# Linear attention feeding a SwiGLU block: group 0's second layer ends tile by tile, batch 1's small matmuls are gathered, batch 1's tail moves into group 1, and one eviction moves to ScalarE

## The chip, the cores and the metric

One NeuronCore of one Trainium2 chip runs the whole program. The metric is device microseconds (us) of one execution; lower is better. Where a ratio is given with an interval, it is a 95% interval.

## The reference, cut to what matters

```python
# q, k, v: 8 batches x 8 heads x 576 positions x 64, float32
q_p, k_p = phi(q), phi(k)                       # phi(x) = elu(x) + 1
kv  = einsum('bhsd,bhse->bhde', k_p, v)         # one 64 x 64 matrix per head
z   = sum(k_p, axis=2)
num = einsum('bhsd,bhde->bhse', q_p, kv)
den = einsum('bhsd,bhd->bhs', q_p, z) + 1e-6
x   = (num / den)  -> 4608 tokens x 512
out = (silu(x @ w_gate) * (x @ w_val)) @ w_out  # 512 -> 1536 -> 512
```

## The kernel before: the parts that matter

The 4608 tokens are worked in nine groups of 512 (`g` = 0 to 8). A group has a *first layer* (12 blocks `fb`, each four gate and four value matmuls of 128x128 by 512 columns) and a *second layer* (four output tiles `t` of 12 matmuls each, evicted from PSUM by ScalarE, "A", or VectorE, "V"). Between these large matmuls the attention of the coming group is done with small ones. A batch has nine blocks of 64 positions and a group takes eight, so group 0 has the first eight blocks of batch 0, group 1 the last of batch 0 and the first seven of batch 1, and the last two blocks of batch 1, its **tail**, belong to group 2.

PSUM is used as four pairs of banks that go round in a ring. `corners` computes numerators (with `R`, the k.v matrices) or denominators (with `Zr`, the sums of k) for a stretch of blocks, as 64x64 matmuls. `kv_corner` computes k.v, `r_copy` copies it out of PSUM into `R`. `lnrd` makes the reciprocal of the denominators on ScalarE (log, then exponential of its negative). `xmul` multiplies numerators by it and writes `xT`, the input of the first layer.

```python
def corners(ps, W, b, lp, j0, j1, c0):           # 4 small matmuls a call
    for l2 in range(2):
        rows = slice(D * l2, D * l2 + D)
        for hh in range(2):
            nc.tensor.matmul(out=ps[l2][C*hh:C*hh+C, c0:c0 + C*(j1-j0)],
                             lhsT=W[rows, lp, hh, :], rhs=qt(b, lp, hh, j0, j1)[rows], ...)
def kv_corner(b, lp, t, first, last):            # 36 matmuls into columns D*lp .. D*lp+63 of BOTH banks
    ...
def block(g):                                    # ahead of the last tile of a group's second layer
    ...
    for lp in range(2):
        num(b1, lp)                              # numerators of the next group
        x_copy(b1, lp, "AV", 2 * C if b1 == 2 else 0)
    if b2 < B:
        kv_all(b2)
        r_copy(b2, 0, 2, "AA")
    ...
def layer2_0():                                  # group 0's second layer, batch 1's attention in between
    ...                                          # dz, cq: the two free pairs of banks
    def s5(): kvr(0)                             # kvr(lp): kv_corner(1, lp), then r_copy of it on VectorE
    def s6(): kvr(1); nx(0, cq)                  # nx: numerators into the pair, then xmul to xT
    def s7():
        nx(1, dz)
        for lp in range(2):                      # the tail of batch 1
            corners(cq, Zr[1], 1, lp, 7, 9, P * lp)
            corners(cq, R[1], 1, lp, 7, 9, 256 + P * lp)
        ...
    step = {1: [s0], 3: [s1, s3], 6: [s2], 7: [s4], 9: [s5], 10: [s6], 11: [s7]}
    for fb in range(FB):                         # all four tiles advance together
        for f in step.get(fb, []): f()
        for t in range(4): l2_mm(0, t, fb)
    s8()                                         # four evictions in a row on VectorE, then the tail's xmul
# group 1 and later, second layer:
for t in range(4):
    ...
    lay2(g, t)
    l2_out(g, t, "AV"[t % 2])                    # tile 1: VectorE
```
(cut and shortened; `...` marks cuts)

## Time and profile before

The median is 319.05 us (318.77 to 319.06, three runs). TensorE is busy 97% of the span.

The first view is a table of windows of the kernel before: one row per stretch, with its length, then the busy time of TensorE (PE), its weight loads (PEld), VectorE (DVE), ScalarE (ACT) and GpSimd (POOL), the granted clock, the DMA share (which this view can print above 1) and the rate. I put the cuts at four marks of the PE timeline: the start of group 0's second layer, of group 1's first layer, of group 1's second layer, and of group 2's first layer.

```profile
core 0: us, PE busy (x) PEld busy (x) DVE busy (x) ACT busy (x) POOL busy (x), PEclk, DMA share, GB/s
39.46:54.59 15.13, 15.05 (x211) 6.85 (x210) 9.36 (x21) 11.46 (x17) 7.10 (x11) 1.00 1.22 206
54.59:75.42 20.83, 20.83 (x98) 9.49 (x97) 20.52 (x38) 11.74 (x20) 3.80 (x6) 1.00 1.09 210
75.42:89.41 13.99, 12.95 (x202) 6.42 (x201) 10.89 (x20) 8.29 (x13) 0.00 (x0) 1.00 0.44 89
89.41:318.50 229.09, 224.93 (x1402) 104.41 (x1399) 141.33 (x231) 95.87 (x149) 14.47 (x21) 1.00 0.36 71
```

One reading aid: PE's ends are modelled and matmuls overlap, so I count a piece of work from its start to the next start. Four large matmuls then take 0.86 us.

Next, the waits of PE from 38 to 92 us in the kernel before (who waited, for whom: total, times, longest).

```profile
PE pp L252 <- DVE osb L320: 1.0, 1, 1.0
```

And the PE timeline of the kernel before around the places that the change touches (start, length, line, operands, shape, count; in brackets the idle time before it and what ended it). L297 is the second layer, L290 the first, L183 k.v, L252 the corners.

```profile
49.85 0.48 PE L183 MATMUL pp<-vr,kp 64*64 64x64 f16 x36
50.26 1.04 PE L297 MATMUL pp<-wo,hT 128*128 128x512 f16 x4
51.23 0.48 PE L183 MATMUL pp<-vr,kp 64*64 64x64 f16 x36
51.53 0.40 PE L252 MATMUL pp<-qT,R 64*64 64x64 f16 x8
51.86 1.04 PE L297 MATMUL pp<-wo,hT 128*128 128x512 f16 x4
52.83 0.42 PE L252 MATMUL pp<-qT,R 64*64 64x64 f16 x8
53.07 0.55 PE L252 MATMUL pp<-qT,Zr 64*64 64x128 f16 x4
53.38 0.29 PE L252 MATMUL pp<-qT,R 64*64 64x128 f16 x4
...
53.72 1.04 PE L297 MATMUL pp<-wo,hT 128*128 128x512 f16 x4
54.59 1.02 PE L290 MATMUL pp<-xT,wg 128*128 128x512 f16 x4
...
84.12 0.51 PE L252 MATMUL pp<-qT,R 64*64 64x384 f16 x6
85.67 0.35 PE L252 MATMUL pp<-qT,R 64*64 64x384 f16 x2 [1.04 <-DVE osb L320]
85.68 1.09 PE L183 MATMUL pp<-vr,kp 64*64 64x64 f16 x72
86.70 2.76 PE L297 MATMUL pp<-wo,hT 128*128 128x512 f16 x12
```

Two things are worth seeing. From 50.26 to 51.23 stand four large matmuls in 0.97 us instead of 0.86: each insertion of small work costs about 0.1 us on top of itself. And the block in group 1 takes 2.58 us (84.12 to 86.70), with a hold of 1.04 us until VectorE has evicted output tile 1, whose pair of banks the numerators of the second half are to go into.

### The profile page before, as it was taken

To read this page: it belongs to the slowest core of one execution; us is meant where nothing else is said; L and a number is where in the kernel's file an instruction comes from. 1 tells how busy PE (TensorE), PEld (TensorE's weight loads), DVE (VectorE), ACT (ScalarE), POOL (GpSimd) and SP (SyncE) were. 2 spreads that over 40 slices of the span, in tenths; PEclk is the share of its full clock that TensorE was granted. 3 is DMA by queue.
4 is the path that set the end of the run, shared out by engine and by line. 5 is a ranking of instruction groups with operands and counts; after the bars stand their busy time and mean duration, and the time that the engine had idled before them with its cause. 6 is when DMAs were issued, how large, how long until landed. Compare 5 with 4: busy or idle time off the path is not lost.

```text
span 318.5 us, 5777 instructions
## 1 busy us (share of the span) xinstructions
PE 309.6 (97%) x2315; PEld 147.7 (46%) x2315; DVE 203.7 (64%) x354; ACT 150.8 (47%) x227; POOL 48.4 (15%) x73
## 2 busy tenths in 40 slices
PE   8799999999899999999999999999999999999994
PEld 7544444444444454444444454445444444444443
DVE  3654875999849874988499739973992343234320
ACT  3764859737543474347533753385331333133311
POOL 8565344400000050006000600000000000000000
PEclk9989999999999999999999999999999999999999
DMA  8999999994430389038903790215013400140014
GB/s 158 193 198 199 206 207 206 244 225 89 93 78 3 74 117 234 5 76 119 236 2 67 114 236 16 51 31 127 2 37 70 101 0 2 34 100 0 2 33 99
DMA packets 41163, 32.52 MB, mean 102 GB/s; under 512 B 16432, under 2 KB 36400, under 8 KB 41136
## 3 DMA queue, kind: packets, MB, share of 16 engines
q0 software_dynamic: 20736, 18.58, 37.6%
q1 hardware_dynamic: 20320, 13.51, 17.8%
q8 instruction: 18, 0.29, 0.4%
q10 hardware_dynamic: 80, 0.07, 0.1%
q14 instruction: 9, 0.07, 0.1%
HBM read 37.75 MB, written 9.44 MB: 148 GB/s over the span
## 4 chain that ended last, share of the span: by engine, by line
PE 89%; DVE 5%; DMA 3%; issue 1%; POOL 1%; ACT 0%; POOLq 0%; DVEq 0%
PE pp L290 55%; PE pp L297 27%; DMA vr<-in_v_dram 3%; PE pp L183 2%; PE pp L252 2%; PE pp L274 1%; DVE hT L283 1%; DVE den L218 1%; DVE qp L227 1%; PE pp L122 1%; DVE kp L157 0%; POOL kr L101 0%; DVE prod L214 0%; DVE osb L320 0%; PE pp L368 0%
## 5 line engine op out<-in xcount | busy, mean ns | idle before, releaser
L118 ACT ACTIVATE sil<-pp 128x512 f16<-128x512 f32 x108 | 63.3, 597 | 102.8 <-PE pp L290 97.9
L290 PE MATMUL pp<-xT,wg 128*128 128x512 f16 x424 | 108.9, 380 | 0.0
L290 PE MATMUL pp<-xT,wv 128*128 128x512 f16 x424 | 108.9, 380 | 0.0
L283 DVE SCALAR_TENSOR_TENSOR hT<-pp,sil 128x512 f16<-128x512 f32 x108 | 72.0, 681 | 47.4 <-PE pp L290 34.3
L297 PE MATMUL pp<-wo,hT 128*128 128x512 f16 (+1 forms) x444 | 97.5, 374 | 0.5 <-DVE osb L320 0.5
L297 PEld LDWEIGHTS <-hT 128*128 128x128 f16 x444 | 42.1, 98 | 48.8 <-issue 1.9
L290 PEld LDWEIGHTS <-wv 128*128 128x128 f16 x424 | 41.4, 98 | 50.1
L290 PEld LDWEIGHTS <-wg 128*128 128x128 f16 x424 | 41.4, 98 | 49.4
L320 DVE TENSOR_SCALAR osb<-pp 128x512 f32<-128x512 f32 (+1 forms) x20 | 13.2, 674 | 31.4 <-PE pp L297 31.4
L118 ACT ACTIVATE osb<-pp 128x512 f32<-128x512 f32 (+1 forms) x17 | 9.8, 578 | 34.9 <-PE pp L297 34.9
L118 ACT ACT_TABLE_LOAD x14 | 18.0, 1283 | 2.8 <-PE pp L290 2.6
L118 ACT ACTIVATE ek<-kr 128x1152 f16<-128x1152 f16 x16 | 17.8, 1155 | 0.3 <-DMA kr<-in_k_dram 0.3
L644 POOL COPY gate<-qT 128x1 f16<-128x1 f16 x4 | 1.4, 359 | 102.4 <-DVE hT L283 75.8
L227 DVE TENSOR_TENSOR qp<-qp,rden 128x1152 f16<-128x1152 f16 x12 | 16.2, 1347 | 0.0
L218 DVE TENSOR_REDUCE den<-prod 128x18 f32<-128x1152 f16 x12 | 16.1, 1343 | 0.0
L118 ACT ACTIVATE eq<-qr 128x1152 f16<-128x1152 f16 x12 | 13.2, 1147 | 0.0
L269 DVE TENSOR_SCALAR xT<-pp 128x512 f16<-128x512 f32 (+1 forms) x14 | 8.8, 667 | 6.8 <-PE pp L252 6.8
L101 POOL DMA_DIRECT2D vr<-in_v_dram x16 | 11.7, 734 | 6.6 <-DMA wo<-in_moe_w_out_dram 1.9
L101 POOL DMA_DIRECT2D kr<-in_k_dram x16 | 11.5, 720 | 6.6 <-DMA wo<-in_moe_w_out_dram 1.9
L101 POOL DMA_DIRECT2D qr<-in_q_dram x15 | 10.9, 731 | 8.5 <-DMA vr<-in_v_dram 2.5
L145 DVE TENSOR_SCALAR ek<-ek 128x1152 f16<-128x1152 f16 x16 | 7.5, 471 | 5.4 <-ACT ek L118 5.4
L157 DVE TENSOR_TENSOR kp<-ek,kp 128x1152 f16<-128x1152 f16 x14 | 10.6, 758 | 0.5
(66 smaller groups left out, 180.6 us busy)
## 6 DMA issues: line engine op xcount, KB each, us to landing
out_dram<-osb SPq DMA_DIRECT2D x70, 128.0 KB, 3.3
kr<-in_k_dram POOLq DMA_DIRECT2D x16, 288.0 KB, 6.7
vr<-in_v_dram POOLq DMA_DIRECT2D x16, 288.0 KB, 10.2
qr<-in_q_dram POOLq DMA_DIRECT2D x15, 288.0 KB, 12.5
wo<-in_moe_w_out_dram POOLq DMA_DIRECT2D x3, 512.0 KB, 13.0
wg<-in_moe_w_gate_dram POOLq DMA_DIRECT2D x5, 256.0 KB, 9.4
wv<-in_moe_w_val_dram POOLq DMA_DIRECT2D x5, 256.0 KB, 9.9
q<-in_q_dram SPq DMA_DIRECT2D x1, 576.0 KB, 3.7
```

The lines of the kernel that those rows point to most:

```text
L101: nc.gpsimd.dma_start(out=dst[b % NB][:, 2 * lp:2 * lp + 2, :], in_=src[b].rearrange("(l a) (c j) d -> (a c) l (j d)", a=2, j=J)[:, 2 * lp ...
L118: nc.scalar.activation(out=out, in_=in_, func=func, bias=bias, scale=scale)
L145: nc.vector.tensor_scalar(out=a, in0=a, scalar1=1.0, scalar2=None, op0=ALU.min)
L157: nc.vector.tensor_tensor(out=a, in0=ek[b % 2][:, lp, :, :], in1=a, op=ALU.add)
L183: nc.tensor.matmul(out=ps[hh][D * l2:D * l2 + D, D * lp:D * lp + D], lhsT=t[b % 2][rows, lp, j, D * l2:D * l2 + D], rhs=vr[b % NB][rows, 2 ...
L218: nc.vector.tensor_reduce(out=den[:, c, :], in_=prod[:, :, :].rearrange("p j (l d) -> p (j l) d", d=D), axis=AX.X, op=ALU.add)
L227: nc.vector.tensor_tensor(out=qv, in0=qv, in1=rden[:, c, :].unsqueeze(2).to_broadcast([P, 2 * J, D]), op=ALU.mult)
L269: nc.vector.tensor_scalar(out=dst, in0=ps[l2][:, c0:], scalar1=1.0 / SC, scalar2=None, op0=ALU.mult)
L283: nc.vector.scalar_tensor_tensor(out=hT[g % 2][:, fb, :], in0=ps[1][:, :], scalar=SC, in1=s[:, :], op0=ALU.mult, op1=ALU.mult)
L290: nc.tensor.matmul(out=ps[h][:, :], lhsT=w[:, c, P * fb:P * fb + P], rhs=xT[g % 2][:, c, :], start=(c == 0), stop=(c == 3))
L297: nc.tensor.matmul(out=l2p[(g, t)][:, n0:n1], lhsT=hT[g % 2][:, fb, P * t:P * t + P], rhs=wo[:, fb, n0:n1], start=(fb == 0), stop=(fb == F ...
L320: nc.vector.tensor_scalar(out=o[:, n0:n1], in0=ps[:, n0:n1], scalar1=1.0 / SC, scalar2=None, op0=ALU.mult)
```

## The change

The intent: end group 0's output tiles one after the other, so that their evictions spread and PSUM pairs come free early; join the two denominators of batch 1 and its two k.v halves, for fewer insertions; open group 1 with two chunks of `xT` for two pairs of banks, so that the second half of `xT` may come later; move batch 1's tail out of group 0 into the block of group 1; and evict tile 1 of group 1 on ScalarE. The tail needs a log there, so the table set with log and exponential is named for that layer.

The diff in full:

```diff
--- before.py
+++ after.py
@@ -520,10 +520,21 @@
         if b1 < NG:
             for lp in range(2):
                 num(b1, lp)
+                if b1 == 2:
+                    corners(nump[(2, lp)], R[1], 1, lp, 7, 9, 0)
                 x_copy(b1, lp, "AV", 2 * C if b1 == 2 else 0)
         if b2 < B:
             kv_all(b2)
+            if b1 == 2:
+                for lp in range(2):
+                    corners(kvp[b2], Zr[1], 1, lp, 7, 9, 2 * P + P * lp)
             r_copy(b2, 0, 2, "AA")
+            if b1 == 2:
+                lnrd(kvp[b2], 0, 2 * P, 4 * P)
+                for lp in range(2):
+                    for l2 in range(2):
+                        w0 = 2 * P + P * lp
+                        xmul(xT[0][:, 2 * lp + l2, 0:P], nump[(2, lp)][l2][:, 0:P], rd[0][:, l2, w0:w0 + P])
         put_off(l2p[(g, "p", 1)])
 
     def layer2_0():
@@ -559,53 +570,41 @@
                 for b in range(2):
                     p8[b][f]()
 
-        def s2():
-            den(0, dz)
-
         def s3():
             qtr(1, 1, cq[1])
             for f in pm[1]:
                 f()
 
         def s4():
+            den(0, dz)
             den(1, cq)
 
-        def s5():
-            kvr(0)
-
-        def s6():
-            kvr(1)
-            nx(0, cq)
-
-        def s7():
-            nx(1, dz)
-            for lp in range(2):
-                corners(cq, Zr[1], 1, lp, 7, 9, P * lp)
-                corners(cq, R[1], 1, lp, 7, 9, 256 + P * lp)
-            exp_k(2, 0)
-            exp_k(2, 1)
-            lnrd(cq, 0, 0, 256)
-
-        def s8():
-            for t in range(4):
-                l2_out(0, t, "V")
-            for l2 in range(2):
-                xmul(xT[0][:, l2::2, 0:P], cq[l2][:, 256:512].rearrange("p (l c) -> p l c", l=2),
-                     rd[0][:, l2, 0:256].rearrange("p (l c) -> p l c", l=2))
-
-        step = {1: [s0], 3: [s1, s3], 6: [s2], 7: [s4], 9: [s5], 10: [s6], 11: [s7]}
-        for fb in range(FB):
-            if fb in step:
-                for f in step[fb]:
-                    f()
+        step = {1: [s0], 3: [s1, s3], 7: [s4]}
+        FO = 8
+        for fb in range(FO):
+            for f in step.get(fb, []):
+                f()
             for t in range(4):
                 l2_mm(0, t, fb)
-        s8()
+        for t in range(4):
+            if t == 2:
+                kvr(0)
+                kvr(1)
+            if t == 3:
+                nx(0, dz)
+            for fb in range(FO, FB):
+                l2_mm(0, t, fb)
+            if t < 3:
+                l2_out(0, t, "V")
+        nx(1, cq)
+        exp_k(2, 0)
+        exp_k(2, 1)
+        l2_out(0, 3, "V")
         exp_q(2, 0)
         exp_q(2, 1)
         phi_k(2, 0)
         phi_k(2, 1)
-        ring[:] = [dz, l2p[(0, "p", 0)], l2p[(0, "p", 1)], cq]
+        ring[:] = [l2p[(0, "p", 0)], dz, cq, l2p[(0, "p", 1)]]
 
     for g in range(NG):
         b1, b2 = g + 1, g + 2
@@ -636,7 +635,15 @@
                     ld2(k, kr, 2)
                     ld2(q, qr, 2)
                     ld2(v, vr, 2)
-            l1(g, fb)
+            if g == 1 and fb < 2:
+                if fb == 0:
+                    two = [pair(), pair()]
+                    for cs in ((0, 1), (2, 3)):
+                        for i in range(2):
+                            l1_mm(g, i, two[i], cs)
+                l1_post(g, fb, two[fb])
+            else:
+                l1(g, fb)
             for f in sl[fb]:
                 f()
         if g + 3 < B:
@@ -654,6 +661,8 @@
                 f()
             for t in range(4):
                 if t == 0 and b2 < B:
+                    if g == 1:
+                        nc.scalar.preload_act_table_set("natural_log_exp_and_others")
                     exp_k(b2, 0)
                     exp_k(b2, 1)
                     exp_q(b2, 0)
@@ -675,7 +684,7 @@
                         o = l2_out(g, t, "V" if n0 == 0 else "A", n0, n1, o)
                     continue
                 lay2(g, t)
-                l2_out(g, t, "AV"[t % 2])
+                l2_out(g, t, "A" if g == 1 and t == 1 else "AV"[t % 2])
             if b2 < B:
                 zb(b2)
```

## The prediction

> **What bounds the kernel.** TensorE. The page has PE busy 97% of 318.5 us; in the timeline four 512-column matmuls repeat every 0.86 us at a granted clock of 1.0. From group 1 on, the table of waits lists only two PE waits: 1.0 us (numerator matmuls of group 2, for an output eviction on VectorE at 84.94) and 0.5 us at the very end. Only PE time outside the large matmuls can be won.
>
> **What the change touches, from the PE timeline.**
>
> 1. Group 0's second layer, 39.46 to 54.59, takes 15.1 us, of which 48 large matmuls are 10.4. The rest is small work in seven insertions, each with about 0.1 us extra when large matmuls resume. The Trainium skill ("TensorEngine Tiling (Array Packing)", Key Properties: mode switching requires a drain) fits: the weight-load row shows 0.42 us of "issue" before each small block. The last insertion (52.83 to 53.72, 0.89 us) contains the 16 tail corners of batch 1, with a hold of 0.38 us that the chain of waits follows to VectorE's xT multiplication, because the corners reuse the bank it reads.
> The change leaves six insertions, joins the denominators and the k.v blocks, and moves the tail away: 0.89 becomes about 0.36, one switch saves 0.1, joining saves 0.1. Estimate -0.7 us. The reordered evictions should not stall PE: by my walk the first half of xT is ready at 53.5 and 54.2 against its use at 53.9 and 54.3, the second at 54.8 and 55.4 against 55.6. That fits only because group 1 opens with two chunks of two pairs; margins are 0.1 to 0.8 us.
>
> 2. The block in group 1's layer 2 (84.12 to 86.70) takes 2.58 us; its sibling in the next group (118.00 to 119.22) takes 1.22. The difference is the 1.04 wait plus a slower k.v run after it. Evicting tile 1 on ScalarE, idle then, removes the wait: -1.3 us.
>
> 3. The moved corners return in this block as 16 matmuls of 64x64x128: by the sibling's 0.46 us for 16 corners, +0.4 us.
>
> 4. New ScalarE work there (two logs and two exponentials of 256 columns, 1.75 us by the earlier trace) and four VectorE multiplications (about 0.27 each) run under the last 12 large matmuls (2.7 us) and end about when group 2's first layer starts, each chunk just in time (margin 0.2 to 0.6). Cost 0 expected, up to 0.5.
>
> 5. The named table load costs nothing: the exponentials needed one load there anyway (1.28 us in the trace). The Trainium skill ("ScalarE: Activation LUTs", Table sets) says that set has both exp and ln, so the later log needs no second one.
>
> Later groups are unchanged and PE-dense, so the shift persists: -0.7 -1.3 +0.4 = -1.6 us; I allow 0.1 for small holds.
>
> **Prediction.** 317.4 us, range 316.7 to 318.3. Faster by over 2%: 0.01; within 2%: 0.98; slower by over 2%: 0.01.
>
> **What would show each step.** Group 1's first layer starts near 53.9 instead of 54.59 (1). PE's wait for the eviction is gone, and the block spans about 1.6 us (2, 3). Group 2's first layer begins near 87.9 instead of 89.41, without a PE wait for xT (4). Table loads stay 15 (5).
>
> **What would make it wrong.** A table load inserted around the late log; xT chunks late at either opening; R copies on VectorE queued behind evictions, holding batch 1's numerators; bank reuse at group 2's start waiting for the last multiplications. Each costs 0.3 to 1.5 us and brings the time back toward 318 to 319. If VectorE's backlog in group 1 was itself delaying PE, the gain could reach 2.2.

## The result, and the profile after

The kernel after takes 317.2 us (317.1 to 317.46, four runs) against 318.91 us (318.47 to 319.06, four runs); the ratio is 0.995 [0.9933, 0.9967]. A ratio is the mean time of one kernel's fast runs over that of the other's of the same rounds, so not quite the ratio of the medians quoted.

The windows of the kernel after, cut at the same four marks:

```profile
36.98:52.45 15.47, 14.85 (x195) 6.88 (x194) 9.90 (x21) 10.66 (x15) 6.42 (x9) 1.00 1.22 207
52.45:73.29 20.84, 20.84 (x102) 9.52 (x98) 20.53 (x37) 10.98 (x18) 5.24 (x8) 1.00 1.19 227
73.29:86.19 12.90, 12.90 (x218) 6.48 (x217) 10.56 (x22) 10.21 (x18) 0.00 (x0) 1.00 0.62 112
86.19:315.30 229.11, 224.95 (x1402) 104.49 (x1400) 141.52 (x232) 95.98 (x149) 14.24 (x21) 1.00 0.36 70
```

The waits of PE from 38 to 92 us in the kernel after:

```profile
PE pp L183 <- DVE R L199: 0.5, 1, 0.5
```

The PE timeline of the kernel after at the places that answer to those shown of before (L274 is the two-chunk opening of group 1's first layer):

```profile
40.39 0.72 PE L376 MATMUL pp<-id,qr 128*64 128x128 f16 x8
40.94 0.61 PE L368 MATMUL pp<-id,qr 128*64 128x128 f16 x16
41.48 3.63 PE L297 MATMUL pp<-wo,hT 128*128 128x512 f16 x16
...
48.30 0.48 PE L183 MATMUL pp<-vr,kp 64*64 64x64 f16 x36
49.28 0.60 PE L183 MATMUL pp<-vr,kp 64*64 64x64 f16 x36 [0.51 <-DVE R L199]
49.82 1.04 PE L297 MATMUL pp<-wo,hT 128*128 128x512 f16 x4
50.79 0.42 PE L252 MATMUL pp<-qT,R 64*64 64x64 f16 x8
51.14 1.04 PE L297 MATMUL pp<-wo,hT 128*128 128x512 f16 x4
52.10 0.41 PE L252 MATMUL pp<-qT,R 64*64 64x64 f16 x8
52.45 0.39 PE L274 MATMUL pp<-xT,wg 128*128 128x512 f16 x1
...
82.09 0.63 PE L252 MATMUL pp<-qT,R 64*64 64x384 f16 x16
82.55 0.83 PE L183 MATMUL pp<-vr,kp 64*64 64x64 f16 x72
83.20 0.30 PE L252 MATMUL pp<-qT,Zr 64*64 64x128 f16 x8
83.43 2.76 PE L297 MATMUL pp<-wo,hT 128*128 128x512 f16 x12
```

The surprise is in the first row. Group 0's second layer, which was to lose 0.7 us, is 0.34 us *longer* (15.47 against 15.13). The gain inside the windows is all in group 1's second layer (13.99 to 12.90), where the wait for the eviction is gone. The other 2.5 us of the difference between the two spans lie before the first mark, in a part of the program whose order of instructions is identical in both. So two questions stood open: what of the time is the change's at all, and what ate the gain in group 0. The new wait of 0.51 us between the two k.v halves is the suspect for the second.

### The profile page after: what moved, and what is told of

Same layout as the page of the kernel before. It is cut to its first block, busy times and chain, and to the rows that moved or that the text cites. A ratio compares the mean times of both kernels' runs of the same rounds, so it can differ in the third digit from the quotient of the medians.

```text
span 315.3 us, 5774 instructions
## 1 busy us (share of the span) xinstructions
PE 307.6 (98%) x2315; PEld 146.9 (47%) x2315; DVE 204.7 (65%) x355; ACT 151.2 (48%) x228; POOL 48.3 (15%) x73
## 4 chain that ended last, share of the span: by engine, by line
PE 85%; DMA 10%; POOL 2%; issue 1%; DVE 0%; ACT 0%; POOLq 0%; DVEq 0%
PE pp L290 51%; PE pp L297 29%; DMA qr<-in_q_dram 4%; DMA kr<-in_k_dram 3%; DMA vr<-in_v_dram 3%; PE pp L252 2%; PE pp L183 1%; PE pp L274 1%; POOL wg L110 0%; POOL wv L110 0%; POOL kr L101 0%; DVE osb L320 0%; POOL qr L101 0%; POOL vr L101 0%; PE pp L210 0%
## 5 line engine op out<-in xcount | busy, mean ns | idle before, releaser
L290 PE MATMUL pp<-xT,wg 128*128 128x512 f16 x416 | 106.8, 379 | 0.0
L290 PE MATMUL pp<-xT,wv 128*128 128x512 f16 x416 | 106.8, 379 | 0.0
L290 PEld LDWEIGHTS <-wv 128*128 128x128 f16 x416 | 40.7, 98 | 49.1
L290 PEld LDWEIGHTS <-wg 128*128 128x128 f16 x416 | 40.6, 98 | 48.6 <-DVE xT L406 0.3
L118 ACT ACT_TABLE_LOAD x13 | 16.7, 1283 | 2.3 <-PE pp L290 2.1
```

What stands on the lines that cost most here:

```text
L118: nc.scalar.activation(out=out, in_=in_, func=func, bias=bias, scale=scale)
L290: nc.tensor.matmul(out=ps[h][:, :], lhsT=w[:, c, P * fb:P * fb + P], rhs=xT[g % 2][:, c, :], start=(c == 0), stop=(c == 3))
```

## The experiments

Twelve runs were made, each with five rounds beside the kernel before on the same chip; two of them repeat the two kernels, and e8 repeats e4. All results were correct. The table has what each came to: time, the ratio to before, and the two stages that the change touches. "q wait" is by how much the stretch of transposes in group 0's layer (the pieces L376 and L368 after the first eight large matmuls) exceeds the 0.79 us it takes when undisturbed; "net" is the layer without it.

| run | time, us | ratio to before | group 0, layer 2 | q wait | net | group 1, layer 2 |
|---|---|---|---|---|---|---|
| first trace of before | 319.05 | | 15.13 | 0 | 15.13 | 13.99 |
| first trace of after | 317.2 | 0.995 [0.9933, 0.9967] | 15.47 | 0.30 | 15.17 | 12.90 |
| c1_before | 318.36 | 0.9987 [0.9965, 1.0009] | 15.13 | 0 | 15.13 | 14.09 |
| c2_after | 317.42 | 0.9957 [0.9935, 0.9978] | 15.17 | 0 | 15.17 | 12.91 |
| e1_evict | 316.92 | 0.9942 [0.9919, 0.9964] | 15.59 | 0.47 | 15.12 | 12.66 |
| e2_tail | 318.11 | 0.9976 [0.9951, 1.0002] | 15.10 | 0.51 | 14.59 | 14.30 |
| e3_noevict | 318.13 | 0.9998 [0.9974, 1.0022] | 15.17 | 0 | 15.17 | 13.64 |
| e4_join | 316.46 | 0.9937 [0.992, 0.9953] | 14.39 | 0.01 | 14.38 | 12.92 |
| e5_plain | 318.3 | 1.001 [0.998, 1.004] | 15.17 | 0 | 15.17 | 12.92 |
| e6_tailevict | 316.69 | 0.9942 [0.9924, 0.9959] | 14.59 | 0 | 14.59 | 12.86 |
| e7_rfirst | 316.97 | 0.9952 [0.9938, 0.9966] | 15.57 | 0.52 | 15.05 | 12.91 |
| e8_join_again | 316.7 | 0.9943 [0.9931, 0.9956] | 14.46 | 0.09 | 14.37 | 12.93 |
| e9_join_qearly | 316.19 | 0.9928 [0.9915, 0.994] | 14.38 | 0 | 14.38 | 12.89 |
| e10_apart | 316.58 | 0.9952 [0.9927, 0.9977] | 14.60 | 0 | 14.60 | 12.90 |

The medians of before were 318.63 (the c runs, e1, e2), 318.56 (e3 to e6), 318.53 (e7 to e9) and 318.38 us (e10). Single runs of one kernel mostly spread over 0.4 to 1.4 us, and a few stand up to 2.4 us above their median (320.76 among the runs of before, for instance), so intervals are as wide as most of the effects here. The six that stand highest are also the six with the lowest mean granted clock, 0.994 or 0.995 where the others have 0.997 to 1.0. They enter the means, so they move ratios: e5 has two of them, e3 and e10 one each, and before has one beside e3 to e6. The stage lengths are far steadier: group 1's first layer is 20.83 to 20.85 us in every trace but e5, and the rest after group 2's opening 229.1 to 229.2. I therefore take the times as a check and decide by stages.

### c1_before and c2_after: both kernels again

The edit is none.

> The kernel before once more, as a control. My theory of where the two traces differ: the first 37 to 39 us are the same program in both, so the 2.5 us by which the first trace of before reaches group 0's second layer later (39.46 against 36.98) is scatter of the loads, not the change. If so, this trace begins that layer somewhere between 36.9 and 39.5, and the layer lasts 15.1 to 15.5 us, the longer the earlier it begins (a wait for the second q load of batch 1, which lands near 40.8). Rival: the change did speed the beginning; then this trace again begins the layer near 39.4. Time 318.5 to 319.1.

> The kernel after once more. Theory: group 0's second layer lasts 15.4 to 15.5 us again if the wait for the copy of R (0.5 us) is part of the program, and the block in group 1 about 1.35 us. The beginning scatters as in the other control. Rival (the change sped the beginning): it begins the layer at 37.0 again while the control of before does not. Time 317.0 to 317.5, ratio 0.995.

Before begins group 0's second layer at 37.53 us this time, not at 39.46, and after at 37.48 instead of 36.98. So the beginning is scatter, and two things made up the 2.5 us. The first trace of before held PE for 1.2 us there for a load of v, and the new one has no such wait. And for some 3 us the clock granted to TensorE was half, as the windows view of the first trace of before shows:

```profile
15.10:18.18 3.08, 3.08 (x86) 1.68 (x85) 1.29 (x2) 2.34 (x4) 2.70 (x4) 0.50 1.45 198
```

The same matmuls take 1.81 us at a clock of 1.00 in the first trace of after (13.95 to 15.76), and 1.81 us in c1. No run shows why the clock was lower. In all twelve experiments the layer begins between 37.09 and 37.55. Comparing the first two spans (318.5 and 315.3) would have credited the change with 2 us that are not its own. The rival is out.

The stage readings repeat: 15.13 and 14.09 for before, 15.17 and 12.91 for after. Group 0's layer is 15.17 us without a wait for q, and the 0.30 us more in the first trace of after were that wait. In this pair the medians differ by 0.94 us and the stages by 1.14.

### e1_evict: only the eviction of tile 1

```diff
 # kernel before
-                l2_out(g, t, "AV"[t % 2])
+                l2_out(g, t, "A" if g == 1 and t == 1 else "AV"[t % 2])
```

> Before with only the eviction of tile 1 in group 1 moved to ScalarE. My theory: the numerator matmuls no longer wait, the block falls from 2.58 to about 1.25 us and the time by 1.1 to 1.3 us (ratio about 0.996). Rival: VectorE's backlog is what holds, so the wait moves to the next thing that VectorE delivers (the x copies) and the gain is under 0.5 us.

In the PE timeline of this run the eight matmuls of the numerators go through without a hold:

```profile
82.42 0.52 PE L252 MATMUL pp<-qT,R 64*64 64x384 f16 x8
```

The block falls from 2.58 to 1.12 us (82.42 to 83.54), with no wait in it, and the layer from 14.09 to 12.66. The median is 316.92 us, 1.7 under before; the layer accounts for 1.4 of that. This one line thus does all that the whole change does: in the same call the change itself measured 317.42. The rival, that the wait would move on to VectorE's copies, is out.

### e2_tail: only the move of the tail

```diff
 # kernel before
         def s7():
             nx(1, dz)
-            for lp in range(2):
-                corners(cq, Zr[1], 1, lp, 7, 9, P * lp)
-                corners(cq, R[1], 1, lp, 7, 9, 256 + P * lp)
             exp_k(2, 0)
             exp_k(2, 1)
-            lnrd(cq, 0, 0, 256)
 # s8: without the tail's xmul; block() and the table load as in the change
```

> Before with only the tail of batch 1 moved into group 1's block (and the named table load), group 0's layer otherwise as before, tile 1 still evicted on VectorE. Theory: group 0's layer loses the 0.38 us hold and 0.2 us of corners, so about 0.5 us shorter; the block in group 1 gains 0.3 to 0.4 us of corners; the wait for the eviction shrinks from 1.04 towards 0.4 because VectorE starts group 1 without 0.75 us of multiplications. Total -0.3 to -0.9 us. Rival: the tail only changes place and its cost stays; total within 0.2 us of before.

Group 0's layer sheds 0.54 us net (15.13 to 14.59), a little over the 0.5 expected. Group 1's layer gets 0.21 longer (14.30 against 14.09). The wait for the eviction did not shrink as I had expected; it is still 1.0 us, although VectorE's multiplications for the tail are gone from group 1's beginning. VectorE ends its sums ahead of that eviction 9.70 us after the layer's start in this trace, as in c1. The median is half a microsecond under before, and the interval reaches 1.

### e3_noevict: the change without the eviction

```diff
 # kernel after
-                l2_out(g, t, "A" if g == 1 and t == 1 else "AV"[t % 2])
+                l2_out(g, t, "AV"[t % 2])
```

> After with tile 1 of group 1 evicted on VectorE again. Theory: VectorE's queue is what the eviction waits in; in the traces of after VectorE ends its sums 0.6 us sooner relative to the layer's start than before, so the wait comes back only in part: about 0.5 us, layer 2 of group 1 about 13.4 us (12.9 in after, 14.0 before), time +0.5 us against after. Rival (the eviction is worth 1.3 us wherever it stands): 14.2 us and +1.3.

The wait is back, but shorter, as the PE timeline of this run shows:

```profile
83.12 0.35 PE L252 MATMUL pp<-qT,R 64*64 64x384 f16 x4 [0.31 <-DVE osb L320]
```

Group 1's layer is 13.64 us, 0.73 over after (12.91): between the two expectations, nearer to mine of 0.5 than to 1.3. The time is 318.13 us, hardly under before. Where e1 won 1.43 us with this line, only 0.73 remain for it when the rest of the change is there. In c2 VectorE ends its sums 9.02 us after the layer's start, 0.68 earlier than in c1. The head start belongs to the reordering: these sums end 9.01 to 9.03 us after the layer's start in every run with the tiles ending one by one, e5 without the two-chunk opening among them, and 9.60 to 9.77 in every run with the old order, e2 and e6 without the tail's multiplications among them. The likely reason is that the evictions of group 0 no longer stand in a row at group 1's opening; no run changes that alone. The head start covers about half of what the eviction on ScalarE is for. The two parts overlap; their gains do not add.

### e4_join: k.v of batch 1 really as one block

```diff
 # kernel after
             if t == 2:
-                kvr(0)
-                kvr(1)
+                kv_corner(1, 0, kp, True, True)
+                kv_corner(1, 1, kp, True, True)
+                r_copy(1, 0, 2, "VV")
```

> After with the two k.v blocks of batch 1 issued back to back and the copies of R after both (VectorE). Theory: the wait of 0.5 us between the blocks, for the first copy queued behind the eviction of tile 1, is the whole reason why group 0's second layer did not get shorter; it goes, the layer takes about 14.65 us plus whatever wait for the q load there is, and nothing else takes its place; time 0.5 us under after. Rival (VectorE is full there; the wait moves to batch 1's numerators or to xT at group 1's opening): the layer stays at 15.1 to 15.2, time as after.

All 72 matmuls run through, and nothing takes the wait's place, in the PE timeline of this run:

```profile
48.33 0.80 PE L183 MATMUL pp<-vr,kp 64*64 64x64 f16 x72
49.07 1.04 PE L297 MATMUL pp<-wo,hT 128*128 128x512 f16 x4
50.03 0.42 PE L252 MATMUL pp<-qT,R 64*64 64x64 f16 x8
```

Group 0's layer is 14.38 us net, 0.79 under after, more than the 0.5 of the wait: the two halves now take 0.74 us where they took 1.52. The idle mark of 0.51 understates what the wait costs, since the second half also runs slower after it: 0.54 us to the next start in after (49.28 to 49.82), 0.41 where it did not wait (e10, 48.65 to 49.06). The median is 316.46 us. The rival is out.

### e5_plain: group 1 opened in the ordinary way

```diff
 # kernel after
-            if g == 1 and fb < 2:
-                ...                    # two pairs, chunks (0, 1) of both, then (2, 3) of both
-            else:
-                l1(g, fb)
+            l1(g, fb)
```

> After with group 1 opened in the ordinary way (all four chunks of one pair at once). Theory: chunks 2 and 3 of xT are ready about 0.8 to 1.0 us after the opening wants them, so PE waits 0.7 to 1.0 us for VectorE's xT multiplication at the opening; time +0.7 to +1.0 against after. Rival (PE reaches the opening late enough): no wait, time as after.

Group 1's first layer takes 21.76 instead of 20.84 us. The PE timeline of this run at the opening:

```profile
52.30 0.76 PE L290 MATMUL pp<-xT,wg 128*128 128x512 f16 x2
53.28 0.38 PE L290 MATMUL pp<-xT,wg 128*128 128x512 f16 x1 [0.22 <-DVE xT L406]
53.88 0.38 PE L290 MATMUL pp<-xT,wg 128*128 128x512 f16 x1 [0.22 <-DVE xT L406]
```

The idle marks say only 0.22 us each because the ends of the matmuls ahead are modelled; start to start, the first four matmuls take 1.80 us (52.30 to 54.10) instead of 0.86. So 0.92 us hang on the two-chunk opening once the tiles end one by one. It wins nothing over before; it repairs what the reordering would break.

### e6_tailevict: the change without the reordering and the opening

This is e2 and e1 together: group 0's layer in its old order, the tail moved, tile 1 evicted on ScalarE.

```diff
 # e2_tail
-                l2_out(g, t, "AV"[t % 2])
+                l2_out(g, t, "A" if g == 1 and t == 1 else "AV"[t % 2])
```

> After without the tile-by-tile ending and without the two-chunk opening: group 0's layer in its old order, but the tail moved to group 1 and tile 1 evicted on ScalarE. Theory (the reordering is a net loss because of the wait for R): group 0's layer about 14.65 us plus the wait for the q load, layer 2 of group 1 about 12.9, so 0.4 to 0.5 us under after. Rival (the reordering was worth its while): slower than after.

Group 0's layer is 14.59 us net and group 1's 12.86. The median is 316.69 us. So the ending tile by tile with its gathered blocks cost 0.58 us of PE in the change as it stood (15.17 against 14.59), and by the stages the kernel is better without it. The medians point the same way, but the intervals of e6 and c2 overlap. Against e1 the tail adds 0.20 us to group 1's layer, for 0.53 off group 0's.

### e7_rfirst: is VectorE's queue what holds the copy?

```diff
 # kernel after
             if t == 2:
                 kvr(0)
                 kvr(1)
+                l2_out(0, 1, "V")
 ...
-            if t < 3:
+            if t in (0, 2):
                 l2_out(0, t, "V")
```

> After with only the order on VectorE changed: the eviction of group 0's tile 1 is queued after the copies of R instead of ahead of them. This tells apart two causes of the 0.5 us wait of the second k.v block. Cause A (as my prediction had it): the copy is late because VectorE is busy with that eviction; then the wait falls to 0.1 us or less and group 0's layer to about 14.75 us. Cause B: the second block writes the same two banks that the copy reads, so back to back it must wait for block end, copy start and copy length whatever VectorE does (0.22 to 0.36 us of copy and the handover); the eviction adds only some 0.15 us; then the wait stays at 0.3 to 0.4 us and the layer at about 15.0 us. I expect B. Time 0 to 0.2 us under after.

The VectorE timeline of this run, at the two copies of R:

```profile
49.29 0.36 DVE L199 CAST R<-pp 128x64 f16<-128x64 f32 x2 [0.67 <-PE pp L183]
50.28 0.36 DVE L199 CAST R<-pp 128x64 f16<-128x64 f32 x2 [0.63 <-PE pp L183]
```

VectorE now stands idle for 0.67 us, waiting for PE to finish the first half. Still PE waits 0.40 us for the copy afterwards (0.51 before this edit), and the layer is 15.05 us net, 0.12 under after. So queueing behind the eviction, which is the cause my prediction had named as a risk, is worth 0.1 us; the handover from PE to VectorE and back is worth 0.4 of idle PE, and 0.67 of the layer (15.05 against 14.38 in e4).

### e10_apart: large matmuls between the halves

```diff
 # kernel after
+            if t == 1:
+                kvr(0)
             if t == 2:
-                kvr(0)
                 kvr(1)
```

> After with the two k.v blocks of batch 1 set apart by four large matmuls (the first ahead of tile 1's end, the second ahead of tile 2's), everything else as in after. Cause B (the handover block, copy, block on the same banks) says that 0.86 us of large matmuls covers it: no wait for R, one more switch of 0.1 us, group 0's layer 14.75 to 14.8 us apart from a wait for the q load, time 0.3 to 0.4 us under after. Rival (something else of the reordering costs the 0.5 us): the layer stays at 15.1 to 15.2 us.

There is no wait for R, and the PE timeline of this run shows the halves around four large matmuls:

```profile
47.25 0.50 PE L183 MATMUL pp<-vr,kp 64*64 64x64 f16 x36
47.68 1.04 PE L297 MATMUL pp<-wo,hT 128*128 128x512 f16 x4
48.65 0.48 PE L183 MATMUL pp<-vr,kp 64*64 64x64 f16 x36
```

The layer is 14.60 us net, even below the 14.75 expected, with one insertion more. It is as long as in e6, which also has seven insertions (14.59), while e4 with six has 14.38: one insertion costs about 0.2 us in all, twice the 0.1 that shows in the large matmuls beside it. So the wait belongs to the close succession of the two halves, and to nothing else of the reordering. The mechanism, as code and traces have it: the first half is copied from columns 0 to 63 of two banks, the second half writes columns 64 to 127 of the same two, each bank is one tile of the program, and the second half waits for the copy as if for the whole bank. The Trainium skill ("PSUM — Partial Sum Buffer", PSUM bank collisions raise a hardware error) asks for this, by bank and quadrant and not by address. The trace agrees that PE waits for a copy of columns it does not write; no run here took the guard away. The kernel before had four large matmuls in that place (50.26 to 51.23) and so never showed the wait.

### e8_join_again and e9_join_qearly: the loads ahead of group 0's layer

```diff
 # e4_join
     ld_w2(0, 4)
     ld(q, qr, 1, 0)
-    ld_w2(4, 8)
     ld(q, qr, 1, 1)
+    ld_w2(4, 8)
     ld_w2(8, 12)
```

> The kernel with both k.v blocks ahead of the copies again, as the partner of the next run on the same chip. Layer of group 0 14.4 to 14.6 us, the whole about 316.5.

> The kernel with joined k.v blocks, and the second q load of batch 1 issued ahead of the second third of the output weights instead of behind it. Theory: in runs that reach group 0's second layer early, PE waits up to 0.5 us for that load (its landing near 40.8 us sets the time); with the load ahead the layer lasts 14.35 to 14.4 us in every trace and the median falls by 0 to 0.3 us against the joined kernel. Rival (the loads are limited as a whole, the wait moves to the output weights): no change in time.

The joined kernel repeats with 316.7 us and 14.37 us net. With the q load ahead, the layer shows no wait for q, and the median is 316.19 us (315.94 to 316.37) against 316.42 to 316.84 of its partner on the same chip: the ranges do not overlap. That is 0.5 us, more than the 0.09 us of q wait in the partner's one trace; the q wait varies from 0 to 0.52 us over the traces, and the rest of the difference has no stage in these two traces that shows more than 0.35 us (the start of the layer, 37.20 against 37.55, which scatters). The direction is shown, the split is not. This is the best version found by its median: 0.9928 [0.9915, 0.994] of before.

## Why the prediction was right or wrong, point by point

The time was right: 317.4 us predicted, 317.2 measured, inside the range. But the sum came out right with one wrong term, and the difference of the first measurement flatters it. Over all executions of both kernels (53 of before, 10 of after) the medians are 318.53 and 317.31 us, 1.2 us apart; the first four runs of each gave 1.71, and my sum was 1.6. That 317.4 was hit is luck: the stages gave 1.1 us of the 1.6, and the 0.5 that was missing was made good by a starting value, 319.05, that lies 0.5 above the median of all executions of before.

1. *Group 0's second layer, "Estimate -0.7 us": wrong.* It measured +0.04 us net. The parts were well sized: the tail with its hold was 0.54 us (e2), and joining plus one switch less is 0.21 us (e4 against e6, 14.38 against 14.59); with the halves really joined (e4) the layer is 0.75 us shorter than before, about what was estimated. What failed was the step "joining saves 0.1" as the change is written: it did not join the k.v halves, it put them back to back with a copy out of the same banks in between, and the old order had covered that handover with large matmuls. That cost 0.79 us (after against e4), so the reordering as a whole lost 0.58 (after against e6). I had listed a wait for the copies of R among the dangers, but for another reason (VectorE's queue) and on other matmuls (the numerators); e7 and e10 show that of the 0.5 us for which PE stood idle the queue is 0.1 and the succession 0.4.

2. *The eviction, -1.3 us: right.* The wait is gone and the block shrinks by 1.46 us with this line alone (e1). What I did not see is that the rest of the change would have recovered half of it anyway (e3).

3. *The corners in their new place, +0.4 us: too high.* They cost 0.20 to 0.22 us (e6 against e1, layer and block). The block of after is 1.34 us long, not 1.6.

4. *The new ScalarE and VectorE work under the last large matmuls, cost 0: right, and close.* In c2 the last three multiplications run from 85.85 to 86.54 and the first weights of group 2 wait 0.28 us for `xT`, but the first matmul starts only some 0.05 us late. The opening of group 1 held too, and e5 shows that it needs the two chunks.

5. *The table load costs nothing: right.* There are 16 loads in both traces (the prediction's 15 leave out the one at the program's start). The Trainium skill ("ScalarE: Activation LUTs", Table sets: the hidden batching unit) puts exponential and log into one set, and the trace agrees: the logs and exponentials of 83.88 to 85.62 in after run without a load between.

So the net of the change over its stages is +0.04 in group 0 and -1.09 to -1.18 in group 1, some 1.1 us. The one wait for the eviction of tile 1 is worth more than that (1.43 in e1), so all of it is to be had with e1 alone. But in the whole change the gain is not all the work of the edit to that eviction: without it (e3) the change is still 0.41 us shorter than c1_before by the two stages, through VectorE's head start, though its time shows no gain (0.9998).

## What to carry to other kernels

Gathering small work into one block saves its switches only if the block has no round trip inside: if a part's result must be copied out of a PSUM bank before the next part may write that bank, write all parts first and copy once, or leave large matmuls in between. When several edits are made at once, read each stage's length by itself, since a correct total may hold a gain and a loss that cancel. And before crediting a difference of two spans to a change, cut them at the first instruction that differs.

## What the Trainium skill lacked or had wrong

- "TensorEngine Tiling (Array Packing)", Key Properties, says that a change of tiling mode drains the engine but gives no size. Here the weight-load row is idle for 0.42 us before each small block, and the four large matmuls next to a change take 0.95 to 0.97 us from start to start instead of 0.86: some 0.1 us an insertion there, and about 0.2 in all (14.60 in e10 with seven insertions, 14.38 in e4 with six). No run separates the drain from other costs of the change.
- "PSUM — Partial Sum Buffer", PSUM bank collisions, gives the rule to guard by bank and quadrant but not what it costs in a chain of matmul, copy, matmul on one bank. Here it is 0.51 us of idle PE with VectorE busy, 0.40 with VectorE free (0.79 and 0.67 us of the layer against the joined halves), and none with four large matmuls (0.97 us) in between.
- "ScalarE: Activation LUTs", What ACT_TABLE_LOAD costs, adds a drain of about 1380 ns to the load's 1283 ns, 2.66 us for a switch. The load measures 1283 ns here, but at the load looked at the drain does not show: in the ScalarE timeline of after, the Silu ahead ends within 0.01 us of the load's start and the next exponential starts 1.29 us after it.

```profile
72.63 0.60 ACT L118 ACTIVATE sil<-pp 128x512 f16<-128x512 f32 x1 [1.13 <-PE pp L290]
73.24 1.28 ACT L665 ACT_TABLE_LOAD   x1
74.53 2.22 ACT L118 ACTIVATE ek<-kr 128x1152 f16<-128x1152 f16 x2
```
